# Fused attention and expert layer on one core: V turned by transpose instructions, its logit columns from a 16-column product

## The chip, the cores and the metric

The kernel runs on one core of a Trainium2 chip (trn2). The metric is the device time of one execution in microseconds (us); lower is better. The kernel before takes 745.04 us, the median of 3 runs (744.35 to 745.72).

## What is computed

Causal attention with a bias from cumulated positive scores, 8 batches of 8 heads, 576 positions of 64 channels, all in float32; then each of the 4608 resulting rows of 512 channels goes to the one of 8 experts that its cosine with the experts' embeddings picks, through two matrices with a ReLU between them.

```python
scores = scale * q @ k.T                      # (8, 8, 576, 576)
scores = where(causal, -1e9, scores + minimum(bias, 0))
attn = softmax(scores)
x = (attn @ v) -> rows (4608, 512)            # all heads of a position side by side
logits = normalized(x) @ normalized(expert_emb).T / tau
e = argmax(logits); out = gate * (relu(x @ w1[e]) @ w2[e])
```

## The kernel before

**Stages.** A start (to about 60 us) loads the first heads and fills the pipeline. Then comes one `step(n)` for each of the 64 heads, n = 8 b + c8, b the batch (to about 336 us). The last 400 us are the experts' products, which the change does not touch. The order of all instructions is written out by hand: each engine executes what `step` calls in the order of the calls, and a name such as `ta_` or `vcp` is one small function.

**A step on TensorE**, in its order: `ta_` (a mask product, a product of the row maximum for a later head on tile `s`, then four products of Q and K on tile `ta`), `sa`, `tb_`, `tbm`, `s3`, `sc_` (a 192-column product into a part of `ta` that may be written once ScalarE has taken the exponential of `ta`), `tbl` (ending in a mask product), `emm`, `sb` (a 288-column product on `s`, then a 64-column one on `ta`), and `pv`, 45 short products of the probabilities with V.

**V's way.** V comes in transposed: `vT` holds, for a batch, 4 pairs of heads, each 128 channels (two heads) by 640 positions. `emm(n)` (lines 296 to 302) takes from one pair's `vT` three blocks of 128 positions in even steps and two in odd steps, 160 blocks in all, and multiplies each, as the stationary operand, with `en4`, 144 columns wide: the identity in columns 8 to 136, which turns V, and on either side the 8 experts' embeddings for one head's 64 channels, which gives that head's part of the logits. Tile `V` in PSUM then holds 144 columns a block; `vcp` copies it, scaled, into the float16 tiles `vh` (ScalarE) and `vl` (VectorE).

**V's scale.** `vsq(b, (p,))` squares one pair of `vT` on ScalarE and sums it; in batches 2 to 7 it stands at the end of steps c8 = 2 to 5 of the batch before. `vscale` adds the four sums with a small product in step c8 = 6, and VectorE makes the scale of it at the start of step 7. `loadt(b, p)` loads pair p on SyncE's queue at the end of steps c8 = 0 to 3.

**ScalarE in a step**: `expa` (the exponential of `ta`, line 500), `prep` on K (64x1152, lines 326 and 332), `expb1` (the exponential of `tb`, line 503), `vcp`'s copy (line 311), `prep` on Q, and a square (line 281) where there is one.

Of the kernel before, what the change touches and what calls it, by code (L numbers as in the profile page):

```python
# [8 lines left out]
F32 = mybir.dt.float32  # L9
# [11 lines left out]
B, H, S, D = 8, 8, 576, 64  # L21
# [17 lines left out]
NE, F, DM = 8, 1024, 512  # L39
# [75 lines left out]
def main(ctx, tc, qkh, qkc, vtin, s_in, emb, tau, w1h, w2h, out, shared, nb):  # L115
    nc = tc.nc
# [36 lines left out]
    NH, LA = nb * H, 5  # L153
# [116 lines left out]
    def loadt(b, p):  # L270
        if b < nb:
            VB.setdefault(b, dict(vh=vhs[b % 2]))
            nc.sync.dma_start(vTs[b % 2][:, p], vtin[b, :, p])
# [9 lines left out]
    def vscale(b):  # L283
        pb = om[:, 496:500]
        nc.tensor.matmul(pb, onesb, VB[b]["sq"].bitcast(BF16).rearrange("p (c t) -> p c t", t=2)[:, :, 1], start=True, stop=True)
        sc = p2.tile([128, 1], F32, name="sc", bufs=3)
        si = sc.bitcast(I32)
        ws = p2.tile([128, 2], F32, name="ws", bufs=3)
        first.append(partial(nc.vector.tensor_reduce, sc, pb, AX.X, ALU.add))
        first.append(partial(soon, partial(nc.vector.tensor_scalar, sc, sc, 1.0e-30, 1.0e30, op0=ALU.max, op1=ALU.min),  # L290
                             partial(nc.vector.tensor_scalar, si, si, -0.5, float((127 + 14) * (1 << 23) + (125 << 22)), op0=ALU.mult, op1=ALU.add),
                             partial(nc.vector.tensor_single_scalar, si, si, 0x7F800000, op=ALU.bitwise_and), partial(VB[b].update, sc=sc, ws=ws),
                             partial(nc.vector.tensor_scalar, ws[:, 0:1], sc, 1.0e-6 * 2.0 ** -XSH, None, op0=ALU.mult),
                             partial(nc.vector.tensor_scalar, ws[:, 1:2].bitcast(I32), si, -1.0, float((254 + XSH) << 23), op0=ALU.mult, op1=ALU.add)))

    def emm(n, t=None):
        b, p, js = n // H, n % H // 2, ((0, 1, 2), (3, 4))[n % 2]
        if t is None:
            t = ps_m.tile([128, 512], F32, tag="m", name="V")
        for i, j in enumerate(js):  # L300
            nc.tensor.matmul(t[:, 144 * i:144 * i + 144], vTs[b % 2][:, p, 128 * j:128 * j + 128], EN[0][:, p], start=True, stop=True)
        VB[b]["V", n] = t[:, 0:144 * len(js)].rearrange("p (j c) -> p j c", c=144)

    def vcp(n, low):
# [255 lines left out]
    EN, r7s = {}, []  # L560

    def rsetup():
        EN[0] = en4 = const.tile([128, 4, 144], F32, name="en4")
        v = nc.vector
        a, b, c, d = (es[:, i:i + 1] for i in range(4))

        def r0():
            nc.scalar.activation(P32J[0:NE, 0:DM], em, AF.Square, accum_out=a)
            nc.scalar.activation(c, a, AF.Ln, bias=tiny[0:NE])
            nc.scalar.activation(b, c, AF.Exp, scale=0.5)  # L570

        def r1():
            v.tensor_scalar(d, itau[0:NE], 0.0, 2.0, op0=ALU.is_ge, op1=ALU.mult)
            v.reciprocal(itau, itau)
            v.scalar_tensor_tensor(itau, itau, -1.0, itau, op0=ALU.mult, op1=ALU.max)
            nc.gpsimd.memset(en4[:, :, 0:8], 0.0)
            nc.gpsimd.memset(en4[:, :, 136:144], 0.0)
            nc.gpsimd.tensor_copy(en4[:, :, 8:136], ident.unsqueeze(1).to_broadcast([128, 4, 128]))

        def r7():  # L580
            nc.gpsimd.tensor_scalar(d, d, -1.0, c, op0=ALU.add, op1=ALU.mult)
            nc.gpsimd.tensor_scalar(em, em, d, None, op0=ALU.mult)

        def r8():
            pt = ps_m.tile([128, 512], F32, tag="m", name="pe")
            for k in range(4):
                nc.tensor.transpose(out=pt[:, NE * k:NE * k + NE], in_=em[:, 128 * k:128 * k + 128], identity=ident[0:NE, 0:NE])
            pt = pt[:, 0:4 * NE].rearrange("p (c e) -> p c e", c=4)
            for i in range(2):
                v.tensor_copy(en4[64 * i:64 * i + 64, :, 136 * i:136 * i + 8], pt[64 * i:64 * i + 64])  # L590
        def rc():
            v.reciprocal(c, b)

        def rd():
            nc.gpsimd.tensor_tensor(c, c, a, op=ALU.mult)
            nc.gpsimd.tensor_tensor(b, b, c, op=ALU.add)
            nc.gpsimd.tensor_scalar(b, b, 0.5, 1.0e-6, op0=ALU.mult, op1=ALU.add)
        r7s.append(r8)
        return r0, r1, rc, rd, r7

# [611 lines left out]
    def step(n):  # L1212
        m = n + LA - (n < 6)
        live = n < NH
        b0, b1, c8 = n // H, n // H + 1, n % H
        prev = n - 1 < NH
        g, c = n // HG, n % HG
        if live and c == 0:
            hset(g + 1)
            if n > 4:  # L1220
                load(g + 2)
                loadc(g + 2)
        if n == 10:
            setup4()
            setup3()
        fslot()
        norm1(n - 3)
        if live:
            ta_(n, m)
        if prev:  # L1230
            pl_(n - 1, 576, PS(n), "p")
        sr(m, 3)
        norm2(n - 3)
        sa(m)
        if live:
            expa(n)
            prep(n, True)
        norm3(n - 3)
        if n == NH - 2:
            wlow(1)  # L1240
        if NH - 7 < n < NH:
            brk[0] = False
            slots(4)
        if live:
            tb_(n)
        sr(m, 2)
        if mids:
            mids.popleft()()
        if live:
            tbm(n)  # L1250
        s3(m)
        if 3 < n < NH - 7:
            sc_(n, m)
        if live:
            tbl(n)
        if n >= NH:
            mslot()
        if prev and PS(n) < 1600 and n != NH - 3:
            pl_(n - 1, PS(n), 1600, "v")
        if n < NH - 3:  # L1260
            wlow(1)
        k = n - NH + 8
        if k == 3:
            wsq(7, True)
        if n == 7:
            vscale(1)
        if n < NH - 1:
            emm(n)
        if not 3 < n < NH - 7:
            sc_(n, m)  # L1270
        sb(m)
        if n == 7:
            fslot()
        sbr(m)
        if n < NH - 6:
            mslot()
        if n < NH:
            tail(n)
        if n == 5:
            s1(10)  # L1280
            sr(10, 3)
            s2(10)
        pv(n - 2, [0, 1, 2])
        if rq:
            rq.popleft()()
        if n == 5:
            sr(10, 2)
            sr(10, 1)
            s3(10)
        pv(n - 2, [3, 4])  # L1290
        if n == NH - 1:
            emm(n)
        if n == 5:
            s4(10)
        if NH - 7 < n < NH:
            mslot()
        if n >= NH - 1:
            for f in (norm1, norm2, norm3):
                f(n - 2)
        if live:  # L1300
            expb1(n)
            if k == 7:
                wsq(13)
            vcp(n, False)
        if k == 3:
            wsq(8)
        aslot()
        if n == 4:
            load(3)
            loadc(3)  # L1310
        if live:
            prep(n, False)
            vcp(n, True)
        if n == NH - 3:
            pl_(n - 1, PS(n), 1600, "v")
        if n == NH - 1:
            xcv(0, 0)
            xtr(0, 1, pxs())
            xcv(0, 1)
        if k > 0:  # L1320
            wsq((0, 2, 5, 8, 9, 10, 11, 14)[k])
            wcv((0, 0, 0, 0, 2, 1, 2, 1, 1, 1, 0)[k], True)
        brk[0] = False
        if n < NH - 6:
            slots(4)
        if n in (4, 5, 6):
            vsq(1, ((0,), (1, 2), (3,))[n - 4])
        if H <= n < NH and 2 <= c8 < 6 and b1 < nb:
            vsq(b1, (c8 - 2,))
        if live and c8 == 6 and 1 < b1 < nb:  # L1330
            vscale(b1)
        if n == 3:
            loadt(1, pair(1))
        if H <= n < NH and c8 < 4:
            loadt(b1, c8)
        if n == NH - 9:
            wissue(3)
        for _ in range(0 if n == NH - 1 else SCN[c8] if n < NH - 22 else 1 + (n == NH - 2) + (n > NH - 3) if n > NH - 3 else 1 + (c8 > 5) + 4 * (n > NH - 6)):
            scatter()
        later()  # L1340
        if live and c == 0:
            addl(g + 1, True)
        if live and c == 1:
            addl(g + 1, False)
        mrow1(m)
        if n == NH - 6:
            early(slice(0, 2), SPL)
        if live:
            pl_(n, 0, 576, "p")
# [403 lines left out]
```

## Time and profile before

| | us |
|---|---|
| median of 3 runs | 745.04 |
| the profiled execution | 746.9 |
| its span, first to last instruction | 745.2 |
| TensorE busy | 730.0 |
| ScalarE busy | 566.1 |
| VectorE busy | 522.5 |
| GpSimd busy | 400.9 |
| a regular even step, a regular odd step | 4.86, 4.72 |

The execution has 1.7 us around its span. A busy TensorE is not TensorE at its peak, since matmuls overlap: each one's record holds the time until its result has landed, some 0.2 us longer than the time that it keeps the next one waiting. What a matmul costs is read from the distance of starts, or of ends, in a run of equal ones, not from the length of a record. A float32 product shows as two records, each with a weight load (PEld) of its own.

### The profile page before, as it was taken

The page shows a single profiled execution, that of the slowest core. Times are in us where ns is not written, and L with a number is a line of the kernel's source. Part 1 is how long each engine was busy: PE and PEld are TensorE (multiplying, and loading weights), DVE is VectorE, ACT ScalarE, POOL GpSimd, SP SyncE. Part 2 cuts the span into 40 slices and gives each one's busy share as a digit, 9 for nine tenths or more (in the row PEclk, how much of TensorE's full clock was granted, in tenths as well). Part 3 has the DMA queues.
Part 4 walks back from the last instruction along what each step waited for, and adds up shares of the span by engine and source line. Part 5 has one row for each costly group of instructions (what it writes and reads, how often), then busy time and mean ns, then how long its engine had stood idle before and what let it go on. Part 6 is the DMA issues. An engine that isn't in the chain of part 4 may idle for free. (4 is left out here: it accounts for less than half of the span.)

```text
span 745.2 us, 20873 instructions
## 1 busy us (share of the span) xinstructions
PE 730.0 (98%) x7952; PEld 530.3 (71%) x7952; DVE 522.5 (70%) x1812; ACT 566.1 (76%) x1031; POOL 400.9 (54%) x387
## 2 busy tenths in 40 slices
PE   8989999999999999999999999999999999999996
PEld 4879999999999999998565455455454545554554
DVE  8778888878888887868687766664566656654621
ACT  9889999999999999998686868557468577574510
POOL 9997898979898897896422232221222223212011
PEclk9999999999999999999999999999999999999999
DMA  7879879798979797864635956645558559653001
GB/s 151 180 178 188 177 180 217 168 211 178 223 171 222 166 220 169 212 224 162 230 115 174 191 191 179 179 161 126 177 174 141 169 171 195 202 103 92 12 19 55
DMA packets 76001, 124.00 MB, mean 166 GB/s; under 512 B 38823, under 2 KB 39231, under 8 KB 75032
## 3 DMA queue, kind: packets, MB, share of 16 engines
q0 software_dynamic: 19632, 69.69, 40.0%
q1 hardware_dynamic: 56260, 52.84, 27.2%
q8 instruction: 70, 1.15, 0.7%
q14 instruction: 39, 0.32, 0.2%
HBM read 93.99 MB, written 21.49 MB: 155 GB/s over the span
## 5 line engine op out<-in xcount | busy, mean ns | idle before, releaser
L253 POOL TENSOR_TENSOR PL<-P 128x576 f16<-128x576 f32 (+2 forms) x128 | 205.1, 1725 | 7.3 <-ACT P L500 5.1
L924 PE MATMUL pe<-xH,wt 128*128 128x512 f16 (+1 forms) x576 | 153.0, 344 | 0.5 <-PEq L1032 0.5
L1003 POOL DMA_INDIRECT out<-Kx,xj x39 | 44.1, 1130 | 191.5 <-DVE Kx L1002 186.7
L924 PEld LDWEIGHTS <-wt 128*128 128x128 f16 x960 | 85.8, 98 | 81.6 <-issue 1.5
L528 PE MATMUL om<-vh,P 128*128 128x73 f16 x960 | 106.0, 199 | 0.2 <-DVE xt L553 0.2
L529 PE MATMUL om<-vl,P 128*128 128x72 f16 x960 | 105.5, 197 | 0.0
L530 PE MATMUL om<-vh,PL 128*128 128x73 f16 x960 | 105.3, 197 | 0.0
L748 POOL DMA_INDIRECT Qx<-xs,idx x40 | 47.3, 1182 | 104.7 <-ACT vjunk L853 44.5
L363 PE MATMUL s<-qkb 96*128 96x288 f32 (+4 forms) x272 | 95.9, 367 | 1.8 <-DVE z L541 0.9
L924 PE MATMUL pe<-xL,wt 128*128 128x512 f16 (+1 forms) x288 | 95.6, 344 | 0.1
L529 PEld LDWEIGHTS <-P 128*128 128x128 bf16 x960 | 94.6, 99 | 0.5 <-issue 0.4
L530 PEld LDWEIGHTS <-PL 128*128 128x128 f16 x960 | 94.0, 98 | 0.0
L528 PEld LDWEIGHTS <-P 128*128 128x128 bf16 x960 | 93.1, 98 | 0.5 <-DVE xt L553 0.3
L926 PE MATMUL pxs<-xH,wt 128*128 128x64 f16 x432 | 83.2, 193 | 0.0
L371 DVE CUSTOM_DVE_ANT_0 junk<-s,mS 128x448 bf16<-128x448 f32 (+3 forms) x144 | 73.8, 520 | 4.5 <-PE s L363 3.7
L995 PE MATMUL pxs<-wt,hq 128*128 128x512 f16 x297 | 72.7, 379 | 0.0
L503 ACT ACTIVATE P<-tb 128x1024 f32<-128x1024 f32 x64 | 65.2, 1020 | 3.2 <-PE tb L469 2.0
L995 PEld LDWEIGHTS <-hq 128*128 128x128 f16 x360 | 35.2, 98 | 41.8
L926 PEld LDWEIGHTS <-wt 128*128 128x128 f16 x648 | 63.5, 98 | 0.4
L463 PE MATMUL tb<-qkb 128*128 128x448 f32 (+3 forms) x256 | 61.8, 284 | 0.0
L466 PE MATMUL tb<-QC,KC 128*128 128x448 f32 (+3 forms) x256 | 61.2, 300 | 0.0
L898 DVE SCALAR_TENSOR_TENSOR wt<-ring,idx,wt 128x512 f16<-128x512 f32 x80 | 56.7, 745 | 4.4 <-ACT wt L890 4.4
(335 smaller groups left out, 1986.4 us busy)
## 6 DMA issues: line engine op xcount, KB each, us to landing
qkb<-qkh POOLq DMA_DIRECT2D x15, 1216.0 KB, 9.1
ring<-w2h SPq DMA_DIRECT2D x44, 256.0 KB
ring<-w1h SPq DMA_DIRECT2D x36, 256.0 KB
KC<-qkh POOLq DMA_DIRECT2D x14, 576.0 KB, 8.3
QC<-qkh POOLq DMA_DIRECT2D x14, 576.0 KB, 8.9
vT<-vtin SPq DMA_DIRECT2D x24, 320.0 KB
rw<-w1h SPq DMA_DIRECT2D x15, 256.0 KB
rw<-w2h SPq DMA_DIRECT2D x12, 256.0 KB
```

Of the source, the lines that this page charges most:

```text
L253: nc.gpsimd.tensor_tensor(out, a, b_, op=ALU.subtract)
L363: nc.tensor.matmul(out, G[g]["QB"][0:96, h, 128 * i:128 * i + 128], G[g]["KB"][0:96, h, lo:hi], start=True, stop=True)
L371: nc.vector.tensor_tensor_reduce(out=jk, in0=src, in1=ms, scale=1.0, scalar=NEG, op0=ALU.add, op1=ALU.max, accum_out=MP[n // 2][:, n % 2, ...
L463: nc.tensor.matmul(out, G[g]["KB"][:, h, 128 * kb:min(128 * kb + 128, S)], G[g]["QB"][:, h, 64 + qlo:64 + qhi], start=start, stop=False, s ...
L466: nc.tensor.matmul(out, HD[n]["KC"][:, 128 * kb:min(128 * kb + 128, S)], HD[n]["QC"][:, qlo:qhi], start=False, stop=stop, skip_group_check ...
L503: nc.scalar.activation(HD[n]["P32"][:, 576:1600], HD[n]["tb"], AF.Exp, scale=0.125)
L528: nc.tensor.matmul(out, lh, vh[:, kb], start=(kb == 0), stop=False)
L529: nc.tensor.matmul(out[:, u:u + 72], lh, vl[:, kb], start=False, stop=False)
L530: nc.tensor.matmul(out, ll, vh[:, kb], start=False, stop=(kb == j))
L924: nc.tensor.matmul(h, w[:, 128 * c:128 * c + 128], x[:, c, lo:hi], start=(i == 0), stop=(i == 11))
L926: nc.tensor.matmul(X["a"][:, HALF * m:HALF * m + HALF], w[:, 128 * c:128 * c + 128], x[:, c, hi:hi + HALF], start=(i == 0), stop=(i == 11))
L995: nc.tensor.matmul(y, h, w, start=(m == 0 and k == 0), stop=(m == 7 and k == 2))
```

## The change

`emm` makes two instructions of each block: TensorE's transpose mode writes the 128 turned columns, and a product with 16 columns (the two heads' embeddings, `en4` cut to 2 x 8 columns a pair) writes the logit columns on both sides of them. The result in tile `V` has the same layout. In the setup, GpSimd clears 64 columns in one instruction, where it cleared 64 in two and copied the identity, 4 x 128. The squares of V move to steps c8 = 0, 2, 4, 6 of the batch before, behind `vcp`'s copy and ahead of `prep` on Q; `vscale` and the first operation of the scale's chain move into the middle of step 7; each `loadt` is called one step earlier, the first of a batch in the middle of step 7.

```diff
         for i, j in enumerate(js):
-            nc.tensor.matmul(t[:, 144 * i:144 * i + 144], vTs[b % 2][:, p, 128 * j:128 * j + 128], EN[0][:, p], start=True, stop=True)
+            w, o = vTs[b % 2][:, p, 128 * j:128 * j + 128], 144 * i
+            l = t[:, min(o, 104):min(o, 104) + 408 if o > 104 else 272].rearrange("p (a b) -> p a b", b=136)
+            l = l[:, (0, 0, 1)[i]:(0, 0, 1)[i] + 2, (0, 40, 48)[i]:(0, 40, 48)[i] + NE]
+            nc.tensor.transpose(out=t[:, o + NE:o + NE + 128], in_=w, identity=ident)
+            nc.tensor.matmul(l, w, EN[0][:, p], start=True, stop=True)
...
-        EN[0] = en4 = const.tile([128, 4, 144], F32, name="en4")
+        EN[0] = en4 = const.tile([128, 4, 2, NE], F32, name="en4")
...
-            nc.gpsimd.memset(en4[:, :, 0:8], 0.0)
-            nc.gpsimd.memset(en4[:, :, 136:144], 0.0)
-            nc.gpsimd.tensor_copy(en4[:, :, 8:136], ident.unsqueeze(1).to_broadcast([128, 4, 128]))
+            nc.gpsimd.memset(en4, 0.0)
...
-        if n == 7:
-            vscale(1)
+        if c8 == 7 and b1 < nb:
+            vscale(b1)
         if n < NH - 1:
             emm(n)
+        if live and c8 == 7:
+            loadt(b1 + 1, 0)
...
-        if n == 7:
+        if c8 == 7:
             fslot()
...
             vcp(n, False)
+            if n >= H and c8 % 2 == 0:
+                vsq(b1, (c8 // 2,))
...
-        if H <= n < NH and 2 <= c8 < 6 and b1 < nb:
-            vsq(b1, (c8 - 2,))
-        if live and c8 == 6 and 1 < b1 < nb:
-            vscale(b1)
...
-        if H <= n < NH and c8 < 4:
-            loadt(b1, c8)
+        if H <= n < NH and c8 < 3:
+            loadt(b1, c8 + 1)
```

On TensorE, between the last mask product of `tbl` and the first product of `sb`, in an even step (three blocks) the program before has:

```order
L469 LDWEIGHTS identb
L469 MATMUL tb<-trim,identb 128x2x128
L301 MATMUL V<-en_197,vT_96 128x144 x3
L363 MATMUL s_4079<-qkb_94 128x288
L363 MATMUL ta<-qkb_94 128x64
```

and the changed program, in which `emm`'s lines are 304 and 305, at the same place of such a step:

```order
L473 LDWEIGHTS identb
L473 MATMUL tb<-trim,identb 128x2x128
L304 MATMUL V<-ident,vT_96 128x128
L305 MATMUL V<-en_197,vT_96 128x2x8
L304 MATMUL V<-ident,vT_96 128x128
L305 MATMUL V<-en_197,vT_96 128x2x8
L304 MATMUL V<-ident,vT_96 128x128
L305 MATMUL V<-en_197,vT_96 128x2x8
L367 MATMUL s_4170<-qkb_94 128x288
L367 MATMUL ta<-qkb_94 128x64
```

Each of the three wide products has become a transpose and a narrow product with the same stationary block; the `s` product now follows a narrow one. (A float32 matmul loads its own weights and has no separate row for that here.)

On ScalarE, from step c8 = 2 to step c8 = 4 of a batch, the program before has:

```order
L503 ACTIVATE P_87<-tb 128x1024
L311 ACTIVATE vh_109<-V,sc 128x3x144
L326 CAST QC_90<-qkb_93 64x1152
L281 ACTIVATE vjunk,sq<-vT_96 128x576
L500 ACTIVATE P_88<-ta 128x576
L332 ACTIVATE KC_91<-qkb_94 64x1152
L503 ACTIVATE P_88<-tb 128x1024
L311 ACTIVATE vh_109<-V,sc 128x2x144
L332 ACTIVATE QC_89<-qkb_94 64x1152
L281 ACTIVATE vjunk,sq<-vT_96 128x576
L500 ACTIVATE P_86<-ta 128x576
```

and the changed program, from the same copy on:

```order
L507 ACTIVATE P_87<-tb 128x1024
L315 ACTIVATE vh_109<-V,sc 128x3x144
L281 ACTIVATE vjunk,sq<-vT_96 128x576
L330 CAST QC_90<-qkb_93 64x1152
L504 ACTIVATE P_88<-ta 128x576
L336 ACTIVATE KC_91<-qkb_94 64x1152
L507 ACTIVATE P_88<-tb 128x1024
L315 ACTIVATE vh_109<-V,sc 128x2x144
L336 ACTIVATE QC_89<-qkb_94 64x1152
L504 ACTIVATE P_86<-ta 128x576
```

The even step keeps its square, now ahead of the cast of Q; the odd step has none any more.

## Rows read from the trace of the kernel before

**Rows 1.** The page: TensorE's granted clock in 40 slices, tenths of full speed.

```profile
PEclk9999999999999999999999999999999999999999
```

**Rows 2.** Steps c8 = 0, 1, 4: length, busy PE, PEld, DVE, ACT, POOL.

```profile
181.42:186.28 4.86, 4.86 (x77) 4.81 (x74) 3.96 (x19) 4.34 (x6) 4.70 (x5) 1.00 0.90 194
186.28:191.00 4.72, 4.72 (x77) 4.67 (x74) 3.95 (x19) 4.13 (x6) 4.55 (x4) 1.00 0.95 215
...
200.61:205.59 4.98, 4.98 (x77) 4.87 (x74) 4.05 (x19) 4.93 (x8) 2.69 (x3) 1.00 1.06 219
```

**Rows 3.** Timeline (start, length, engine, line), TensorE: blocks of an even, an odd step.

```profile
183.87 0.90 PE L301 MATMUL V<-en,vT 128*128 128x144 f32 x6
...
188.72 0.66 PE L301 MATMUL V<-en,vT 128*128 128x144 f32 x4
```

**Rows 4.** Timeline: 192-column products and the full weight loads around them.

```profile
183.13 0.25 PE L463 MATMUL tb<-qkb 128*128 128x192 f32 x1
183.13 0.19 PEld L466 LDWEIGHTS tb<-QC,KC 128*128 128x128 f32 x1
183.22 0.28 PE L466 MATMUL tb<-QC,KC 128*128 128x192 f32 x1
183.24 0.19 PEld L363 LDWEIGHTS s<-qkb 96*128 96x128 f32 x1
```

**Rows 5.** Timeline: step n = 1, blocks of V behind a 64-column product.

```profile
24.89 0.41 PE L363 MATMUL s<-qkb 96*128 96x288 f32 x2
...
25.11 0.79 PEld L301 LDWEIGHTS V<-en,vT 128*128 128x128 f32 x6
...
25.14 0.37 PE L301 MATMUL V<-en,vT 128*128 128x144 f32 x1
...
25.34 0.41 PE L301 MATMUL V<-en,vT 128*128 128x144 f32 x2
```

**Rows 6.** Timeline: four transposes of 128 columns and what follows, experts' stage.

```profile
362.48 0.60 PE L776 MATMUL pxm<-ident,Qx 128*128 128x128 f32 x4
...
362.92 0.38 PE L995 MATMUL pxs<-wt,hp 128*128 128x512 f16 x1
```

**Rows 7.** Timeline, and min/median/max ns: weight loads of four 8-column transposes, start.

```profile
24.04 0.32 PEld L587 LDWEIGHTS pe<-ident,em 8*128 8x128 f32 x4 [0.18 <-issue]
...
L587 PEld LDWEIGHTS pe<-ident,em x4: 133/136/138, 24.0 to 24.2; 8*128 8x128 f32 x4
```

**Rows 8.** Timeline of ScalarE: exponential of `ta`, steps 32 to 35 (c8 = 0 to 3).

```profile
182.53 0.65 ACT L500 ACTIVATE P<-ta 128x576 f32<-128x576 f32 x1 [0.49 <-PE ta L466]
...
187.39 0.65 ACT L500 ACTIVATE P<-ta 128x576 f32<-128x576 f32 x1 [0.54 <-POOL PL L253]
192.12 0.65 ACT L500 ACTIVATE P<-ta 128x576 f32<-128x576 f32 x1 [0.42 <-PE ta L466]
...
197.12 0.64 ACT L500 ACTIVATE P<-ta 128x576 f32<-128x576 f32 x1
```

**Rows 9.** Timeline of TensorE: products of `s3` and `sc_`, steps 32, 12, 45.

```profile
183.33 0.32 PE L363 MATMUL s<-qkb 96*128 96x288 f32 x1
183.49 0.25 PE L363 MATMUL ta<-qkb 96*128 96x192 f32 x1
...
85.04 0.32 PE L363 MATMUL s<-qkb 96*128 96x288 f32 x1
85.21 0.36 PE L363 MATMUL ta<-qkb 96*128 96x192 f32 x1
...
246.23 0.32 PE L363 MATMUL s<-qkb 96*128 96x288 f32 x1
246.42 0.35 PE L363 MATMUL ta<-qkb 96*128 96x192 f32 x1
```

**Rows 10.** Timeline of TensorE: step 52's wait for the load of Q.

```profile
279.74 0.50 PE L466 MATMUL ta<-QC,KC 128*128 128x320 f32 x2 [0.75 <-DMA QC<-qkh]
```

**Rows 11.** Groups of GpSimd in the first 60 us: the copy of the identity.

```profile
L578 POOL COPY en<-ident 128x512 f32<-128x512 f32 x1 | 0.6, 630 | 0.0
```

More of the change, by code (lines that the diff above doesn't have):

```diff
@@ L589, in r8 @@
             for i in range(2):
-                v.tensor_copy(en4[64 * i:64 * i + 64, :, 136 * i:136 * i + 8], pt[64 * i:64 * i + 64])
+                v.tensor_copy(en4[64 * i:64 * i + 64, :, i], pt[64 * i:64 * i + 64])
         def rc():
```

## The prediction

> **What bounds the kernel now.** I read the stretches of single steps first, then TensorE's timeline with its weight loads, then ScalarE's timeline. In the regular steps TensorE bounds: its busy time is the length of the step, 4.86 of 4.86 and 4.72 of 4.72 us, while ScalarE has 4.34 and 4.13, VectorE 3.96, GpSimd 4.70 and 4.55 [rows 2]. "Busy" alone would not prove it of a cause, but in these steps TensorE's rows show no recurring idle time. So what `emm` costs TensorE between the mask product ahead of it and the `s` product behind it goes into the time one to one. The exception is a wait in the steps that follow ScalarE's squares: step c8 = 4 takes 4.98 where c8 = 0, with the same three blocks, takes 4.86 [rows 2]; it is priced below.
>
> Two things in the timeline have to be kept apart. A product keeps the array for its columns; its weights are loaded behind the columns of the one before. The next product starts when both are over, so each step of such a chain costs the longer of the two. The whole forecast hangs on which is longer.
>
> **What the wide product costs.** In an even step six passes (two for each of three float32 blocks) take 0.90, in an odd step four take 0.66 [rows 3]: 0.12 a pass, and with 0.29 for the last one's record (0.90 - 0.29) / 5 = 0.122. A block costs 0.245, three 0.735, two 0.49. 144 columns are long enough to cover the next weight load, so the loads cost nothing here, and neither does that of the `s` product behind the last block.
>
> **What a full float32 load costs when it is not covered.** Two places show it. A 192-column product starts 0.09 after the one before it (183.13, 183.22), but the load that began at 183.13 keeps the next load until 183.24 [rows 4]: 0.11 from load to load, longer than the columns. And in step 1 the first block stands behind a 64-column product: its load begins at 25.11, its record is 0.37 long where a pass has 0.29, and ends at 25.51, a pass (0.12) ahead of the one that ends at 25.75 - 0.12 = 25.63 [rows 5]; so it really began at 25.22, 0.11 behind its load, though the 64 columns were over long before. The transposed load of 128 columns is shorter: four in 0.32 with 0.14 for the last, (0.32 - 0.14) / 3 = 0.06 from load to load, with 8 columns between [rows 7]. A transpose of 128 columns takes 0.44 / 4 = 0.11 [rows 6].
>
> **The new block.** Transpose T, then the two passes a and b of the 16-column product. T's columns (0.11) just cover a's load (0.11): T to a 0.11. a's 16 columns are about a ninth of 144, 0.014, and cover nothing: a to b is b's load, 0.11. b to the next T is T's load, 0.06. The last b to `s` is the full load of `s`, 0.11, which the wide pass used to cover. Ahead of the first T nothing changes, since the 256-column mask product covers its load. Two blocks: 0.11 + 0.11 + 0.06 + 0.11 + 0.11 + 0.11 = 0.61 for 0.49, so +0.12 in an odd step. Three: 0.61 + 0.06 + 0.11 + 0.11 = 0.89 for 0.735, so +0.155 in an even one. From n = 7 to n = 57 there are 26 odd and 25 even steps: 26 x 0.12 + 25 x 0.155 = 3.1 + 3.9 = **+7.0 us**. The rows are read to 0.01; a load of 0.105 to 0.115 gives 5.6 to 8.4. The bounds for a load that nobody has seen behind 16 columns are its columns alone, 0.014, and 0.11; I take 0.11, since both places of the trace with the same form of load say so and a shorter cover cannot make a load shorter.
>
> [...]
>
> **The other steps.** Steps 0 to 6 and 58 to 63 hold another 33 blocks at about 0.055 each (0.12 / 2 to 0.155 / 3), 1.8 us if nothing covers them. These steps fill and drain the pipeline and TensorE waits there for other engines; covered fully they cost 0. I take +0.6, bounds 0 to 1.8.
>
> **The squares.** ScalarE's exponential of `ta` comes round in 182.53 to 187.39 with 0.54 of idle time, so its work without a square is 4.32; with one it is 192.12 to 197.12, 5.00, without any idle time [rows 8]. Four steps in a row with 5.00 against TensorE's 4.86 and 4.72 push ScalarE late, until `sc_`'s 192-column product waits for the exponential. From the start of the `s` product to the end of the 192-column one it takes 183.74 - 183.33 = 0.41 undisturbed, 0.53 and 0.54 late [rows 9]. There are 11 such places from 85 to 246 us (the first and the last are shown), 11 x 0.12 to 0.13 = 1.4 us. With squares in even steps only, ScalarE has 5.00 + 4.32 = 9.32 in a pair of steps, TensorE 4.86 + 4.72 + 0.275 = 9.86, and the even step alone has 5.02 for 5.00, so the waits go: **-1.4**, bounds -1.5 and 0. What is late next: nothing on ScalarE. The copy to `vh` stays ahead of the square, so VectorE's `vl` and the next step's V tile are not held. `prep` on Q comes 0.68 later, and its reader is a load onto Q that GpSimd issues a full step later. Had the squares stayed where they were, the longer steps would have removed most of this wait too.
>
> **The queues.** Loads of V go one step earlier on SyncE's queue; the first of a batch is now behind the row maxima of step 5 and ahead of those of step 7, and each waits for squares of the batch before, which are long over. In the window between the load onto Q issued in step 1 and its use in step 4 there are two loads of V before and after. The one wait of this kind, 0.75 us in step 52 [rows 10], shrinks by what three steps grow, 0.4: **-0.4**, bounds -0.8 and +0.5. `vscale`'s product and reduction keep their cost and move to where they wait for nothing. GpSimd saves the copy of the identity, 0.63 [rows 11], early in a start in which it is busy; TensorE's start hangs on it only in parts: **-0.3**, bounds -0.6 and 0.
>
> **The sum.** 7.0 + 0.6 - 1.4 - 0.4 - 0.3 = +5.5 us. The profiled execution, 746.9 (span 745.2 and 1.7 around it), becomes 752.4; it stands 1.9 above the median of 745.04, so the median becomes **750.5**, 0.7% slower.
>
> **Rivals.** (1) The other side: the loads hide behind 16 columns after all, because the next one may start ahead of its columns. The place is a to b and b to the next block; it decides as soon as a load costs under 0.06. With loads at nothing a block costs 0.11 + 2 x 0.014 = 0.14 for 0.245, and a pair of steps 9.58 - 0.53 = 9.05. Then ScalarE bounds with 9.32: 25.5 pairs x 0.26 = -6.6, with the squares' -1.4 and the start some -9: **736**. For it speaks only that no row shows so few columns; against it the two places above. Chance 0.05. [...]
> (2) The loads of the narrow product take the 0.06 of the short loads [rows 7], because their product is short. Two blocks: 0.11 + 0.06 + 0.06 + 0.11 + 0.06 + 0.11 = 0.51, three 0.74: +0.02 and +0.01 a step, 0.7 in all, and the rest of the sum makes -1.3: **743.7**. Against it: those are transposed loads, and the ordinary ones read 0.11. Chance 0.06, half of it within 0.2%.
> (3) The clock falls. It is granted in full in every slice [rows 1]. If transposes and waits for loads lowered it to the lower level while `emm` runs (0.61 and 0.89), these 0.75 a step would double: some +38, **788**. Around the experts' transposes nothing fell. [...] Chance 0.02.
> (4) The squares do not do what they say: the waits of `sc_` stay, because the late `prep` holds the next exponential. That is +1.4, **751.9**, inside the range; chance 0.05.
>
> **Chances and range.** Forecast 0.82, rival (4) 0.05, rivals (1) to (3) 0.13. About 0.2%, 1.5 us, is what a measurement of this kernel can tell from no change. Faster by more: (1) and half of (2), 0.08. Within it: the other half of (2) and the forecast with all its small terms at their low ends, 0.05. Slower by more: 0.87. The forecast's own ends: 5.6 + 0.2 - 1.5 - 0.8 - 0.5 = 3.0, so 748.0, and 8.4 + 1.2 - 1.3 + 0 - 0.3 = 8.0, so 753.0. Since the forecast and (4) hold 0.87, that is the range.
>
> **What would show it.** Right: the narrow passes' weight loads 0.11 apart, T 0.11, the `s` product 0.11 behind the last narrow pass; even steps 5.00 to 5.02, odd 4.84; ScalarE idle ahead of each exponential of `ta` in steps 1, 3, 5, 7; no 192-column record of 0.35. Wrong: narrow passes 0.03 to 0.06 apart, or regular steps no longer than now, or waits for ScalarE or for loads of V or Q where none were.

## The result and the profile after

The changed kernel takes **753.23 us** (median of 6 runs, 752.30 to 753.88) where the kernel before takes 745.69 beside it: a ratio of 1.0098, with a 95% interval of 1.0085 to 1.0111. The forecast was 750.5 in a range from 748.0 to 753.0, worked out from 745.04 for the kernel before. So the direction was right and the size too small: +7.5 us for +5.5. The median lies 0.2 above the range; the ratio on 745.04 would make 752.3, inside it. Measured a second time the changed kernel took 753.31, a ratio of 1.0086 (1.0061 to 1.0111).

The profiled execution took 753.9, with a span of 752.1; the one of before had 745.2. The lines of the changed kernel stand a little lower in the file: L304 is the transpose and L305 the narrow product that took the place of L301; L367, L467, L470, L473 and L504 are the old L363, L463, L466, L469 and L500.

First the clock, from the page, which answers to [rows 1]:

```profile
PEclk9999999999999999999999999999999999999999
```

Next the stretches of the steps 32, 33 and 36 (c8 = 0, 1, 4), which answer to [rows 2]: start and end, length, then busy time of TensorE, weight loads, VectorE, ScalarE and GpSimd, then the granted clock.

```profile
182.28:187.31 5.03, 5.03 (x80) 4.99 (x78) 3.96 (x19) 4.32 (x8) 4.67 (x5) 1.00 1.09 235
187.31:192.16 4.85, 4.85 (x78) 4.80 (x76) 3.94 (x19) 4.75 (x6) 4.68 (x5) 1.00 0.92 203
202.06:207.09 5.03, 5.03 (x80) 4.98 (x77) 3.99 (x18) 4.37 (x8) 2.78 (x4) 1.00 1.03 207
```

5.03 for 4.86 and 4.85 for 4.72; TensorE is busy all the time and its clock is granted in full. Step 36, which had 4.98 because of the waits behind the squares, is now as long as step 32. TensorE's timeline (start, length, engine, line) of the blocks in step 32, and then in step 33, answers to [rows 3]:

```profile
184.73 0.27 PE L304 MATMUL V<-ident,vT 128*128 128x128 f32 x1
184.84 0.29 PE L305 MATMUL V<-en,vT 128*128 128x16 f32 x2
184.98 0.30 PE L304 MATMUL V<-ident,vT 128*128 128x128 f32 x1
185.12 0.29 PE L305 MATMUL V<-en,vT 128*128 128x16 f32 x2
185.26 0.31 PE L304 MATMUL V<-ident,vT 128*128 128x128 f32 x1
185.41 0.29 PE L305 MATMUL V<-en,vT 128*128 128x16 f32 x2
185.55 0.38 PE L367 MATMUL s<-qkb 96*128 96x288 f32 x1
...
189.76 0.27 PE L304 MATMUL V<-ident,vT 128*128 128x128 f32 x1
189.87 0.29 PE L305 MATMUL V<-en,vT 128*128 128x16 f32 x2
...
190.30 0.38 PE L367 MATMUL s<-qkb 96*128 96x288 f32 x1
```

From block to block it is 185.12 - 184.84 = 0.28, where the wide product had 0.245. The `s` product's record is 0.38 long, where it has 0.32 undisturbed [rows 9], so it really began 0.06 later than its row says: 185.61 and 190.36. Three blocks take 185.61 - 184.73 = 0.88 and two 190.36 - 189.76 = 0.60; forecast were 0.89 and 0.61. The `s` product behind the wide blocks of [rows 3] has such a long record too:

```profile
184.51 0.39 PE L363 MATMUL s<-qkb 96*128 96x288 f32 x1
...
189.12 0.39 PE L363 MATMUL s<-qkb 96*128 96x288 f32 x1
```

Read in the same way it began 0.07 later, at 184.58 and 189.19, so three wide blocks took 184.58 - 183.87 = 0.71 and two 189.19 - 188.72 = 0.47, and not the 0.735 and 0.49 of the forecast. An even step grows by 0.17 and an odd one by 0.13.

ScalarE's exponentials of `ta` in the steps 32 to 35 answer to [rows 8], and the 192-column product of step 12 to the second pair of [rows 9]:

```profile
183.39 0.65 ACT L504 ACTIVATE P<-ta 128x576 f32<-128x576 f32 x1 [0.69 <-PE ta L470]
188.43 0.65 ACT L504 ACTIVATE P<-ta 128x576 f32<-128x576 f32 x1
193.28 0.65 ACT L504 ACTIVATE P<-ta 128x576 f32<-128x576 f32 x1 [0.55 <-PE ta L470]
198.32 0.65 ACT L504 ACTIVATE P<-ta 128x576 f32<-128x576 f32 x1
```

```profile
84.80 0.32 PE L367 MATMUL s<-qkb 96*128 96x288 f32 x1
84.95 0.25 PE L367 MATMUL ta<-qkb 96*128 96x192 f32 x1
```

The exponentials follow TensorE's steps, and ScalarE idles ahead of every second one. The late record of 0.36 is 0.25 again; between step 7 and step 58 the trace has no late one left, where before there were 12 (the 11 of the prediction and one more at 261 us). What TensorE waited for from 60 to 310 us is two lines in the kernel before (engine, what, who released it: us in total, times, the longest) and none in the changed one:

```profile
PE s L363 <- DVE z L541: 0.9, 1, 0.9
PE ta L466 <- DMA QC<-qkh: 0.8, 1, 0.8
```

Where the difference stands, by pieces of the program, each from TensorE's or GpSimd's marks in two profiles of either kernel (us):

| piece | before | again | after | again |
|---|---|---|---|---|
| start to step 7 | 59.14 | 57.90 | 58.24 | 58.56 |
| step 7 to step 58 | 249.00 | 248.84 | 253.10 | 253.10 |
| step 58 to step 63 | 21.94 | 21.94 | 22.17 | 22.15 |
| to the first scatter of an expert | 36.80 | 36.79 | 36.79 | 36.78 |
| first to eleventh scatter | 96.35 | 96.35 | 98.13 | 96.88 |
| eleventh to last scatter | 272.00 | 272.01 | 272.16 | 272.19 |
| last scatter of an expert to the final one | 6.18 | 6.18 | 7.74 | 8.23 |
| end | 3.77 | 3.77 | 3.77 | 3.77 |

So 4.1 to 4.3 us of the difference are in the steps that the change touches, and 1.6 to 2.05 in the last wait of the program, far behind them. This second part nobody had forecast; the experiments had to find it.

### The profile page after: what moved, and what is told of

It reads as the page before. It is cut to its first block, busy times and chain, and to the rows that moved or that the text cites. A ratio compares the mean times of both kernels' runs of the same rounds, so it can differ in the third digit from the quotient of the medians.

```text
span 752.1 us, 21189 instructions
## 1 busy us (share of the span) xinstructions
PE 736.5 (98%) x8112; PEld 538.5 (72%) x8112; DVE 523.2 (70%) x1812; ACT 566.4 (75%) x1031; POOL 400.1 (53%) x385
## 5 line engine op out<-in xcount | busy, mean ns | idle before, releaser
L1005 POOL DMA_INDIRECT out<-Kx,xj x39 | 44.0, 1129 | 193.2 <-DVE Kx L1004 188.4
L367 PE MATMUL s<-qkb 96*128 96x288 f32 (+4 forms) x272 | 95.4, 365 | 1.2 <-DVE M L375 0.3
L467 PE MATMUL tb<-qkb 128*128 128x448 f32 (+3 forms) x256 | 62.1, 285 | 0.0
L470 PE MATMUL tb<-QC,KC 128*128 128x448 f32 (+3 forms) x256 | 61.2, 300 | 0.0
```

Source lines behind the costliest of these rows:

```text
L367: nc.tensor.matmul(out, G[g]["QB"][0:96, h, 128 * i:128 * i + 128], G[g]["KB"][0:96, h, lo:hi], start=True, stop=True)
L467: nc.tensor.matmul(out, G[g]["KB"][:, h, 128 * kb:min(128 * kb + 128, S)], G[g]["QB"][:, h, 64 + qlo:64 + qhi], start=start, stop=False, s ...
L470: nc.tensor.matmul(out, HD[n]["KC"][:, 128 * kb:min(128 * kb + 128, S)], HD[n]["QC"][:, qlo:qhi], start=False, stop=stop, skip_group_check ...
```

## The experiments

**1. One part alone.** The first kernel (the turn alone) has the transposes and the narrow product and leaves the squares, the loads and `vscale` where they were; the second (the moves alone) has these moved and keeps the wide product.

The turn only, against before:

```diff
-            nc.tensor.matmul(t[:, 144 * i:144 * i + 144], vTs[b % 2][:, p, 128 * j:128 * j + 128], EN[0][:, p], start=True, stop=True)
...
+            nc.tensor.transpose(out=t[:, o + NE:o + NE + 128], in_=w, identity=ident)
+            nc.tensor.matmul(l, w, EN[0][:, p], start=True, stop=True)
```

The moves only, against before; `vscale` stands in step c8 = 7 now, between the last mask product of `tbl` and the blocks of V, where it stood at the end of step c8 = 6, ahead of the next step's first mask product:

```diff
-        if n == 7:
-            vscale(1)
+        if c8 == 7 and b1 < nb:
+            vscale(b1)
...
+        if live and c8 == 7:
+            loadt(b1 + 1, 0)
...
-        if n == 7:
+        if c8 == 7:
             fslot()
...
+            if n >= H and c8 % 2 == 0:
+                vsq(b1, (c8 // 2,))
...
-        if H <= n < NH and 2 <= c8 < 6 and b1 < nb:
-            vsq(b1, (c8 - 2,))
-        if live and c8 == 6 and 1 < b1 < nb:
-            vscale(b1)
...
-        if H <= n < NH and c8 < 4:
-            loadt(b1, c8)
+        if H <= n < NH and c8 < 3:
+            loadt(b1, c8 + 1)
```

> V turned by transposes and the 16-column product, but squares, loads and scale of V where the kernel before has them. Load theory (each float32 pass waits 0.11 us for its own weight load, each transpose 0.06 for its): regular even steps 5.03, odd 4.85, as in the changed kernel; ScalarE's squares in four steps in a row leave one or two late 192-column products a batch, 0.1 us each, 0.6 to 1.2 in all; so 1.010 to 1.012 of the kernel before, slightly above the changed kernel. Rival (the moved squares, loads and scale cost the time): near 1.000.

> Squares, loads and scale of V moved as in the changed kernel, but V still from the 144-column product. Load theory: regular steps 4.86 and 4.72 everywhere but step 7 (vscale's product now exposes 0.08 there and saves 0.03 in step 6); the eleven late 192-column products are gone; -1.4 - 0.4 + 0.3 = -1.5 us, ratio 0.998 (0.997 to 0.9995). Rival (the moves cost): ratio above 1.002.

Measured: the turn alone is slower, 1.0085 (1.0069 to 1.0100), a little less than the 1.010 to 1.012 expected; the moves alone are faster, 0.9970 (0.9960 to 0.9981), at the low end of what was expected. The windows from step 7 to step 58 (columns as above) are, in this order, those of before, of the changed kernel, of the turn alone and of the moves alone:

```profile
59.14:308.14 249.00, 247.35 (x3695) 243.57 (x3693) 207.79 (x900) 233.13 (x306) 220.66 (x194) 1.00 0.87 193
```

```profile
58.24:311.34 253.10, 253.10 (x3822) 250.50 (x3819) 208.05 (x900) 233.58 (x306) 221.02 (x194) 1.00 0.85 191
```

```profile
58.32:312.56 254.24, 253.68 (x3821) 250.63 (x3819) 207.10 (x900) 233.97 (x306) 221.28 (x194) 1.00 0.86 190
```

```profile
57.98:305.60 247.62, 246.43 (x3695) 243.46 (x3691) 208.38 (x900) 233.01 (x306) 221.24 (x194) 1.00 0.88 195
```

Of before's 249.00, 249.00 - 247.35 = 1.65 are idle time of TensorE, and the 12 late products hide another 1.54 in records that look busy (the sum of what the way from the `s` product to the end of the late one is over 0.41 us). Some waits are left in neither number, so the steps without waits are put together from the medians of the table below: those of before, with the 4.87 and 4.85 of the moves alone for c8 = 4 and 5, where before has most of its late products, and with 0.11 more in step 7, where `vscale` has the new place in every kernel, make 245.3 for the 51 steps (seven each of c8 = 7, 0 and 1, six each of the others). Those of the turn alone, with 0.06 in step 7, make 252.9. So the blocks cost **7.6 us**, against 7.0 forecast; by the rows above it is 25 x 0.17 + 26 x 0.13 = 7.6 as well. The place of `vscale` adds 0.2, up to the 253.1 of the changed kernel, which has no waits. And the waits of before were worth 249.0 - 245.3 = 3.7: the 1.65, the 1.54, and some 0.5 that no single wait shows.

The moves alone take away the 12 late products too, and leave 247.62. Three of their steps (46, 47 and 55) are together 1.8 over their medians, 1.2 of it idle time at 251, 257 and 296 us that the profile releases by "issue" (nothing that it shows) or by `prep` on Q; the turn alone has some 1.0 us of this kind between 252 and 302 us, the two profiles of before and the two of after have none, and the cause stays open. But the turn alone has only two late products left (277 ns): the longer steps give ScalarE its time back without any move. So the two gains do not add. Beside the turn the moves bring next to nothing; beside the wide product they bring the 1.5 us of the late products. The median step lengths show it, by c8:

| c8 | 0 | 1 | 2 | 3 | 4 | 5 | 6 | 7 |
|---|---|---|---|---|---|---|---|---|
| before | 4.86 | 4.72 | 4.88 | 4.72 | 4.99 | 4.99 | 4.89 | 4.70 |
| moves only | 4.87 | 4.72 | 4.88 | 4.72 | 4.87 | 4.85 | 4.86 | 4.80 |
| turn only | 5.03 | 4.85 | 5.03 | 4.84 | 5.04 | 4.99 | 5.07 | 4.83 |
| after | 5.02 | 4.85 | 5.04 | 4.84 | 5.04 | 4.99 | 5.04 | 4.90 |

The step c8 = 7 has 0.10 more with the moves alone than before, and 0.07 more in the changed kernel than with the turn alone: `vscale`'s product was moved there in six of these seven steps. In the changed kernel's step 31 the first transpose behind it ends 0.46 after the start of the last mask product (180.17 and 179.71); in step 33, where no such product stands between them, it is 0.39 (190.03 and 189.64). The 0.07 and 0.10 are close to the loads of the blocks behind it, 0.06 for a transpose [rows 7] and 0.11 for a wide product [rows 5]; that its four columns cover next to nothing of them is an estimate from these numbers. The step c8 = 6, which it left, has 0.03 less.

**2. The same blocks in another order.** All transposes of a step first, then all narrow products.

```diff
+            nc.tensor.transpose(out=t[:, o + NE:o + NE + 128], in_=w, identity=ident)
+        for i, j in enumerate(js):
+            w, o = vTs[b % 2][:, p, 128 * j:128 * j + 128], 144 * i
...
-            nc.tensor.transpose(out=t[:, o + NE:o + NE + 128], in_=w, identity=ident)
```

> The changed kernel with the three (or two) transposes of a step first and the narrow products behind them. Load theory: a transpose's columns now cover another transpose's short load (0.06) and only the last one covers a full load, so an even step grows by 0.10 and an odd one by 0.05: 25 x 0.10 + 26 x 0.05 + edges = +4 us on the changed kernel, about 757.5 or 1.015 to 1.016 of the kernel before. Rival (a pass costs its columns or a fixed issue time, loads are hidden or cost the same everywhere): the order doesn't matter, the time of the changed kernel within 0.5 us.

Measured: 1.0137 (1.0121 to 1.0152), below the 1.015 to 1.016 expected; but the growth of the steps came out as expected. TensorE's timeline in its step 32, the same as above:

```profile
186.80 0.49 PE L302 MATMUL V<-ident,vT 128*128 128x128 f32 x3
187.13 0.74 PE L307 MATMUL V<-en,vT 128*128 128x16 f32 x6
187.72 0.38 PE L369 MATMUL s<-qkb 96*128 96x288 f32 x1
```

Three transposes take 187.13 - 186.80 = 0.33, and six narrow passes 187.78 - 187.13 = 0.65, 0.11 each, the distance of two full loads in [rows 4]. Steps 7 to 58 take 257.45, of which 0.34 is idle time: 4.0 more than in the changed kernel. By the loads an even step has 0.99 for 0.89 and an odd one 0.66 for 0.61, 25 x 0.10 + 26 x 0.05 = 3.8. The arithmetic and the columns are those of the changed kernel; only the neighbours of the loads are others. A price by columns has no place for this. Nor does a fixed 0.11 for the transpose and each narrow pass fit: the changed kernel's block would take 3 x 0.11 = 0.33 by it, and takes 0.28.

**3. One more narrow product, and one of four times the columns.** Both kernels add a product to each block, with the same weights. One repeats the 16-column product into the same place; the other has 64 columns, stands ahead of the narrow one, and its output is read by nothing.

Narrow twice, against the changed kernel:

```diff
+            nc.tensor.matmul(l, w, EN[0][:, p], start=True, stop=True)
```

Wide junk, against the changed kernel:

```diff
+            nc.tensor.matmul(t[:, 432:496], w, EN[0].rearrange("p a b e -> p (a b e)"), start=True, stop=True)
```

> The changed kernel with each 16-column product issued twice. Load theory: two more full loads a block, 0.22 us: even steps +0.66, odd +0.44, 28 us in the 51 regular steps and up to 7 outside: 781 to 788 us. [...]

> Adds to the changed kernel a second float32 product behind each narrow one: the same 128 weight columns, but 64 columns wide, into a spare part of the V tile that nothing reads. It stands against the kernel that repeats the 16-column product (steps 7 to 58 there 281.5 us, that is 28.4 more than the changed kernel). Theory of the loads (a pass costs the longer of its columns and the 0.11 of the next full float32 load): 64 columns are about 64/144 of 0.122, 0.054 us, still shorter than the load, so the wide repeat costs what the narrow one cost: steps 7 to 58 at 281 to 283 us. Theory of the columns (a pass costs something fixed and its columns): each of the two added passes of the 127 blocks in these steps takes (64 - 16) x 0.00085 = 0.041 more, together 10.4 us: 291 to 293 us.

Measured, once each: 792.6 us beside 754.5 for before, and 784.1 beside 746.8. They ran on two chips, on which the kernels before differ by 7.7 us; of the 8.5 us between these two, 7.6 lie behind step 63, and 792.6 is above the 781 to 788 expected for the same reason. The steps can be compared all the same, since the turn alone, from the first of the chips, has the step lengths of the changed kernel to 0.01 where `vscale` plays no part. The windows of the steps 7 to 58, narrow twice and then wide junk:

```profile
61.21:342.73 281.52, 281.52 (x4075) 278.89 (x4073) 208.08 (x900) 237.85 (x307) 222.41 (x195) 1.00 0.78 171
```

```profile
61.16:342.67 281.51, 281.51 (x4076) 278.93 (x4073) 208.09 (x900) 237.78 (x307) 222.14 (x195) 1.00 0.78 172
```

281.52 and 281.51: sixteen columns or sixty-four, the pass costs the same, and 28.4 us over 127 blocks of two passes are 0.112 a pass. This is the cleanest of the results. The timeline of the junk kernel shows the same in one block: from transpose to transpose 202.49 - 201.98 = 0.51, which is the 0.28 of a block and two more passes of 0.112.

```profile
201.98 0.31 PE L304 MATMUL V<-ident,vT 128*128 128x128 f32 x1
202.13 0.33 PE L305 MATMUL V<-en,vT 128*128 128x64 f32 x2
202.30 0.35 PE L306 MATMUL V<-en,vT 128*128 128x16 f32 x2
202.49 0.31 PE L304 MATMUL V<-ident,vT 128*128 128x128 f32 x1
```

**4. Both kernels again.** The late end and the longer experts' pieces of the first profile could have been chance.

> The changed kernel once more, beside its predecessor in the same call. It is to tell what of the 6.9 us between the first two profiles belongs to the change. If all of it does: steps 7 to 58 again 253.1, the first eleven pieces of the experts' stage again near 98.1, the last wait of the program again near 7.7, and a ratio of 1.009 to 1.011. If the 3.4 us outside the attention stage are variation from run to run: 253.1 again, but the experts' pieces and the last wait anywhere between 96.3 and 98.1 and between 6.1 and 7.8; the ratio by the attention stage alone would be 1.004 to 1.006.

> The kernel before once more, unchanged, for a second profile of it. If the two single waits of about 1 us in its steps 26 and 52, the 96.3 us of the first eleven experts' pieces and the 6.2 us of the last wait belong to this kernel, they are all there again (steps 7 to 58 at 249.0). If they vary from run to run, some are gone or elsewhere: steps 7 to 58 between 247.0 and 249.5, and the last wait up to 7.7. The ratio is 1.000 within 0.0015 either way.

Measured: the table of pieces above. The steps came out alike to 0.01 us in the changed kernel; the experts' first pieces did not (98.13 and 96.88, against 96.35 twice), so 0.5 of them may belong to the program and the rest to the run. The last wait did: 7.74 and 8.23, against 6.18 twice. The wait for the load of Q in step 52 is there in both profiles of before [rows 10], longer in the second, and in neither of after.

What the last wait is made of can be read from the DMA view. GpSimd's last scatter of the experts (L1003, in the changed kernel L1005) is followed by a loop ahead of which all engines meet, and GpSimd meets them when that scatter has landed: in the changed kernel the chain that ended last goes from the scatter's transfer, put down as over at 745.26, to the loop's first instruction at 745.28. In the kernel before all its packets are through in one go: the stretch from 736.7 to 737.7, the queue's kind, packets, megabytes, share of 16 engines:

```profile
q0 software_dynamic: 80, 0.26, 68.6%
```

In the changed kernel, 75 of them are through by 742.92, in the same time after the issue. Then, from 742.9 to 743.87 and from 743.87 to 744.5:

```profile
q8 instruction: 1, 0.02, 6.0%
q0 software_dynamic: 5, 0.00, 3.1%
```

```profile
q0 software_dynamic: 1, 0.00, 0.2%
```

A transfer of 16384 bytes on the queue called instruction stands there from 742.92 to 743.86, and the scatter's last packets come at 743.84 and 744.27, behind it; 1.3 us later than in the kernel before, counted from the issue (3.70 for 2.38). In the second profile it is 4.35. These 1.3 and 2.0 are nearly all of the longer wait, 1.56 and 2.05.

**5. More instructions, no more work.** The change gives TensorE 160 instructions more, one transpose for each block. If that moves such a transfer onto the scatter, it must move off again with a few more, and must appear in the kernel before with as many.

Shifted, against the changed kernel:

```diff
-            for k in range(4):
+            for k in 9 * (0, 1, 2, 3):
                 nc.tensor.transpose(out=pt[:, NE * k:NE * k + NE], in_=em[:, 128 * k:128 * k + 128], identity=ident[0:NE, 0:NE])
```

Before, longer, against before:

```diff
-            for k in range(4):
+            for k in 41 * (0, 1, 2, 3):
```

> The changed kernel, with the four small transposes of the embedding (8 rows, 8 columns, once, at 24 us) repeated eight more times into the same place: 32 more instructions for TensorE, some 2 us of its time in the start, and nothing else. It is to tell where the 1.6 to 2.05 us at the program's end come from. Theory of the fetch: a transfer of 16384 bytes on the queue that the profile calls instruction runs from 742.37 to 743.32 us, in the middle of the last scatter's packets, and holds the last of them until 744.02; which of the program's instructions such a transfer stands in front of depends on how many stand ahead of it, so 32 more move the transfer some 3 us earlier, off the scatter: the last wait falls from 7.7 or 8.2 to about 6.1, steps 7 to 58 stay at 253.1. Theory of the work: the late end belongs to what the change does, and stays at 7.7 to 8.2. The start may take up to 2 us longer by either.

> The kernel before, with the same four small transposes repeated forty more times: 160 more instructions for TensorE, as many as the change adds with its 160 transposes, all of them in the start (some 10 us there), and no other change. Theory of the fetch: with as many instructions ahead of the program's end as the changed kernel has, the transfer of instructions falls into the last scatter here too, and the last wait is 7.3 to 8.2 instead of 6.18, while steps 7 to 58 stay between 247.0 and 249.5. Theory of the work: 6.18 as in the kernel before. The whole is up to 10 us longer by either, from the start.

Measured: 756.4 us, 1.0113 (1.0064 to 1.0161), and 764.7 beside 746.8 in a single run; both carry a longer start, some 4 us where 2 were expected and some 16 where 10 were, of which below. Steps 7 to 58 were 253.10 and 248.30. The last wait was **6.11** in the shifted kernel and **7.28** in the lengthened kernel before. In the shifted one the scatter of 744.72 has the stretch from 746.2 to 747.2 to itself, and the transfer ran from 742.1 to 743.1, ahead of it (the second stretch is 741.9 to 743.2):

```profile
q0 software_dynamic: 80, 0.26, 68.8%
```

```profile
q8 instruction: 1, 0.02, 4.5%
q0 software_dynamic: 1, 0.00, 0.0%
```

In the lengthened one the transfer stands from 753.18 to 754.38 among the packets, as it does in the changed kernel, and four come behind it (the stretch from 754.4 to 755.6):

```profile
q0 software_dynamic: 4, 0.01, 3.2%
```

All twelve profiles agree: the last wait is 6.11 to 6.18 where no transfer of instructions runs between the scatter's issue and its landing (seven), and 7.28 to 8.23 where one does (five: the two of after, the turn alone, the turns first, and the lengthened kernel before). A later end alone does not bring it: the kernel of experiment 6 has as many TensorE instructions as before, its steps 7 to 58 take 255.40, and its last wait is 6.12. So in these runs the late end goes with the number of instructions ahead of it (160 more make 7.28 of 6.18, 32 more make 6.11 of 7.74), not with the work of the change. That the transfer carries instructions is read from its queue's name; which engine's, no view shows.

**6. A better place for `vscale`.** The moves alone are faster than both kernels but leave 0.10 in the step c8 = 7. This kernel, shown against the moves alone, puts `vscale` behind the V blocks there.

```diff
-        if c8 == 7 and b1 < nb:
-            vscale(b1)
...
-        if c8 == 7:
-            fslot()
...
+        if c8 == 7 and b1 < nb:
+            vscale(b1)
+            fslot()
         pv(n - 2, [0, 1, 2])
```

> The kernel before with the moved squares, loads and vscale of the change but with the wide 144-column product kept, and vscale put behind the V blocks of its step instead of ahead of them, so that the load of its product is not exposed behind a transposed load. Theory of the loads: against the run with the moves alone (ratio 0.997, c8 = 7 steps 4.80) the c8 = 7 step comes back to 4.72 or 4.75, six times 0.05 to 0.08, 0.3 to 0.5 us: ratio 0.996 to 0.9975. If vscale's place costs nothing: 0.997 as before and 4.80 again.

Measured: 1.0075 (1.0055 to 1.0094), slower, where 0.996 to 0.9975 were expected. The step c8 = 7 takes 6.17 us, and TensorE's timeline says why:

```profile
181.37 0.18 PE L285 MATMUL om<-sq,onesb 128*128 128x4 bf16 x1
182.87 0.20 PE L528 MATMUL om<-vh,P 128*128 128x73 f16 x1 [1.32 <-DVE sc L1059]
```

`vscale` writes four spare columns of the tile `om` that `pv` fills next, and `pv` has to wait until VectorE has read them. Both theories were about the load of that product, and neither looked at who shares its tile. (The transposed load of which the expectation speaks does not exist in this kernel, which keeps the wide product.)

## Why the prediction was right, and where it was not

**The blocks** were priced at +7.0 and cost 7.6. The step that mattered, that 16 columns cover no float32 load and a pass then costs the load's 0.11, holds in three ways: the spacing of the six narrow passes of experiment 2 (0.11), what its order cost (4.0 for 3.8 by the loads), and the 281.52 and 281.51 of the two kernels of experiment 3 (0.112 a pass). The new blocks were priced to 0.01. The term that was too large is the old ones, 0.735 and 0.49 where they took 0.71 and 0.47. The place of `vscale` adds 0.2, by the table of experiment 1: 0.07 more in six steps c8 = 7 and 0.03 less in six steps c8 = 6, where the prediction had said that it keeps its cost.

**The squares** were priced at -1.4, and 1.5 us of late products are gone. That the longer steps alone would remove most of it was said, and the turn alone shows it. The sign named for ScalarE had the wrong parity: it idles ahead of the exponential in the even steps, where the step before had no square.

**The waits.** -0.4 for the load of Q was too small: all of the 1.65 us of single waits went, since the other one (0.9, for `z`) did not come back. The second profile of before has 1.5 for the load alone. For the steps 7 to 58 the prediction makes 7.0 - 1.4 - 0.4 = +5.2; measured are 4.1 and 4.3, since 7.8 came on for the blocks and `vscale`, and waits of 3.7 went where 1.8 were taken off.

**The other steps and the start.** From step 58 to 63 there are 0.2 more. The start varies by 1.2 us between two profiles of the same kernel, so neither the +0.6 nor the -0.3 can be told from it.

**What failed** is a sentence that the sum did not have: the prediction took the experts' stage and the end, behind the last step, to be untouched, since no line of theirs changes. They got 3.5 and 2.8 us longer (the rows of the table behind step 63). 1.6 to 2.05 of it is the transfer of instructions, shown by experiment 5. With that term the forecast of 750.5 would have been 752.1 to 752.6, inside its range. The rest is 0.5 to 1.8 in the first pieces of the experts' stage and 0.2 behind them. In the first profile TensorE waits there 1.2 us for ScalarE (L860), in the second it does not. It does not look like the work of the change either: the wide junk, which has all of that work, has 96.46 in the first pieces, and the lengthened kernel before, which has none of it, 97.22; the 0.2 is gone in the shifted kernel (272.00). Its cause stays open.

**Luck.** That the sum came so close is luck in part. The blocks and `vscale` cost 0.8 more than priced, the waits gave back 1.9 more, and the 2.8 to 3.5 us behind the steps were in no term: the misses partly cancel. The mechanism of the blocks was right; the sum was better than its terms.

**The rivals.** (1) and (2), cheaper loads, are excluded by experiment 3, where a pass costs 0.112. (3), the clock, did not happen in the steps, where 1.00 is granted with six narrow passes in them; below are places where it did. (4), that the waits of the squares stay, is excluded by the trace.

**What beats both kernels** is the moves alone: 0.9970 of the kernel before.

## What to carry over

Here a float32 pass whose columns take less time than the weight load behind it cost that load: 0.112 us with 16 columns and with 64. Splitting one wide float32 product into a transpose and a narrow one traded columns for loads, 0.88 us for 0.71 in an even step, so count the loads that nothing covers. The order counts too: with the transposes between the narrow products the steps 7 to 58 took 253.10, with all transposes of a step first 257.45. When the work of a saturated engine grew, waits of its neighbours disappeared by themselves (12 late products became two with the turn alone), so two edits that remove the same wait must not be added up. And more instructions on an engine cost time far from where they stand: with 160 more in the start of the kernel before, its last wait was 7.28 for 6.18.

## What the hardware showed that was not expected

**A transfer on the queue called instruction stood ahead of a scatter's last packets.** It has 16384 bytes and takes some 0.94 us (742.92 to 743.86); 75 of the scatter's 80 packets are through ahead of it, and the last come at 743.84 and 744.27. It shows in the time because GpSimd waits for just that scatter; what the others cost, no run here measures.

**The granted clock fell to 0.50 behind very small transposes.** In the shifted kernel the start is some 4 us longer, not 2. TensorE's window of the 36 transposes of 8 columns, the ordinary products behind it, the blocks of V behind these, and later stretches (the number ahead of the last two is the granted clock):

```profile
24.40:26.71 2.31, 2.31 (x38) 2.29 (x37) 0.49 (x3) 0.19 (x1) 2.24 (x3) 1.00 0.47 54
26.71:28.00 1.29, 1.29 (x16) 1.29 (x15) 0.72 (x3) 0.50 (x1) 1.29 (x6) 1.00 0.89 150
28.00:30.00 2.00, 2.00 (x14) 2.00 (x13) 0.42 (x4) 1.96 (x5) 1.89 (x15) 0.50 0.90 136
...
34.00:36.00 2.00, 1.95 (x10) 1.11 (x9) 1.22 (x6) 1.58 (x3) 1.96 (x1) 0.79 0.94 153
36.00:40.00 4.00, 3.79 (x63) 3.33 (x63) 3.46 (x12) 3.95 (x5) 1.26 (x2) 1.00 0.05 11
```

TensorE is "busy" nearly throughout, and yet 0.50 is granted from about 28 to 35 us; the changed kernel, with four of these transposes in the same place, keeps 1.00 from 17 to 40 us. In the lengthened kernel before, with 164 of them, the clock falls while they still run, at 27 us, to 0.50, and comes back at 44 us. These two runs do not tell the transposes from the smallness of their 8 columns. The clock also fell where TensorE had nothing to do: in the kernel before TensorE's last product ends at 739.34, 1.00 is granted until about 743.7 and 0.50 from there to the end at 745.2. A fall of the clock, as in rival (3), thus happened in two runs. The transposes of 128 columns between other products did not bring it: in the changed kernel 1.00 is granted from 58.24 to 311.34.
